# Ordering TensorE together with the other engines, in two lanes, with refitted planner costs

## The chip, the cores and the metric

The kernel runs on one NeuronCore of a Trainium2 chip, with its five engines: TensorE (PE, matrix products), VectorE (DVE), ScalarE (ACT), GpSimd (POOL) and SyncE (SP), which issues most DMAs. The metric is the device time of one execution in microseconds, the median of several runs.

## The reference

What is computed is one layer: a layer norm, attention with 32 heads over a sliding window of 256 positions, and a gated feed-forward network on the same normalised input, whose SiLU scales the attention's output.

```
B, S, D = 1, 2048, 512;  H = 32; Dh = 16; W = 256;  F = 1792
xn = layernorm(x)                                   # no gain, no bias
q, k, v = split(xn @ wqkv)                          # 32 heads of 16
scores = q @ k.T * 16**-0.5
mask = (idx[:, None] - idx[None, :] >= 0) & (idx[:, None] - idx[None, :] < 256)
s = (softmax(where(mask, scores, -1e9)) @ v) @ wo
b = (silu(xn @ w1) * (xn @ w3)) @ w2
out = x + s * silu(b)
```

## The kernel before

**Tiling.** The 2048 tokens are handled in four token tiles (t) of 512, the 32 heads in four head groups (g) of eight, and each pair (t, g) in two passes (p): 32 units of attention. float32 operands are kept as two float16 parts, a rounded one and what the rounding lost, so that a product takes three float16 matmuls (`XH`/`XL` are the parts of the normalised input). Working tiles of 2 KB a partition, for weights, hidden values and residuals alike, are taken from a pool of 46 `slot` buffers.

**Stages.** `prepare` does the layer norm of a tile on DVE: statistics (L422, L423), then a short serial chain on 128x4 numbers, the reciprocal square root by three Newton steps (L427, L430, L431, three times L434 to L436, L437), then the centring of four 128x512 tiles (L440). PE transposes these (L478) and DVE splits them into `XH` and `XL` (L487, L488). `project` (L550) and `value` (L520) make q, k and v; q and k go to DRAM (`dQ`, `dK`, issued at L566, L567, L569, L570) and come back in the layout of the scores (L582). A unit's first pass multiplies queries and keys (PE, L604) for the row maxima, which DVE takes (L616); its second pass makes the scores (PE, L678), DVE adds the mask (L685), ACT takes the exponential into `pt` (L688), and PE multiplies `pt` with the values into the bank `po` (L706). ACT and DVE bring `po` out into `os` (L716, L719), and SP gathers it (L725, L726), fetches the denominators (L739), stores their reciprocals (L743, L744 on DVE, then L746) and spreads them (L750); POOL multiplies (L316), and ACT and POOL split the result (L755, L316).

The feed-forward part runs beside attention. `gate_up` (PE L937) makes gate and up; ACT and DVE finish the hidden value (L948, L952, L957), ACT and POOL split it (L963, L316). `down` (PE L987) sums over pieces of F in a bank and adds it to an accumulator, on ACT for the first piece (L1002) and on DVE for later ones (L1007). From the second token tile on, down goes over `product` (PE L1040, ACT L1050, DVE L1053), which uses operands of half size prepared on POOL. `total` (PE L1118, the last tile by columns at L1153) applies wo, and DVE joins it with x (L1125 to L1127, L1155, L1156). Weights are measured (squares on ACT, L247 and L837), scaled and split (ACT L319, L320; POOL L316) on the way.

**PSUM.** Four kinds of banks stand in the text by tag: `m0` and `m1`, which dense products use in turn (below "dense banks"), `s` with two buffers for scores and small products, and `po` for the values. A matmul that begins a new tile of a bank waits until the tile before it has been read out.

**What sets the order.** `tile_block` emits the program once, in an order written by hand: between two batches of scores it places a share of dense work, and short helpers wait in a list for so many steps (`later`). After that, `arrange` reads the whole program: which instruction must come before which (from the parts of tiles that they touch, `box` and `meets`), how long each takes (`cost`), how long after its end a reader on another engine can start (`extra`), how long a DMA occupies the pipe (`carry`), and by when each must be done so that PE isn't held up (`deadlines`). `listed` then simulates the five engines. PE's instructions stay in the order of the program. Each other engine takes, among those that can begin, the one with the earliest deadline, unless a more urgent one is about to become ready. After three rounds, each of which knows the ready times of the round before, the best order is fixed by dependencies between neighbours on DVE, ACT, POOL and SP; the engines then run their lists strictly in order, waiting on semaphores. So a planner that takes an operation for shorter or longer than it is places it among the wrong neighbours, and everything behind it on that engine waits.

## Time and profile before

| | |
|---|---|
| median of 3 runs | 819.77 us (819.29 to 821.17) |
| profiled execution, its own time | 821.13 us |
| its span, first to last instruction | 819.3 us |
| mean granted TensorE clock | 0.994 |
| first matmul begins / last matmul ends | 1.05 us / 815.6 us |
| PE busy | 797.9 us, 97% |
| DVE busy | 639.2 us, 78% |
| ACT busy | 435.3 us, 53% |
| POOL busy | 358.7 us, 44% |

A row of the timeline gives the start in us, the length in us, the engine, the line of the kernel, the operation, the output, the inputs, the shape and the number of instructions joined in it; in square brackets stands how long the engine had been idle before it, and what ended that. A row of the windows gives for each stretch its length and then, for PE, the weight loads, DVE, ACT and POOL, the busy time and the number of instructions; behind these come the granted TensorE clock (1.00 is full), the share of the DMA engines and the traffic in GB/s. A row of the waits names the engine and the group that waited, what released it, the total in us, how often, and the longest.

### The profile page before, as it was taken

What the parts mean: (1) busy time and instruction counts of PE and PEld (TensorE: products, weight loads), DVE (VectorE), ACT (ScalarE), POOL (GpSimd) and SP (SyncE); (2) the same over time, 40 slices, a digit from 0 to 9 for tenths busy, and PEclk for the clock granted to TensorE, in tenths of its full rate; (3) what the DMA queues carried; (4) which work ended last, traced back from release to release, by engine and by line L of the source; (5) the groups of instructions that cost most, each with busy time, mean ns of one, the idle gap of its engine ahead of it and who ended that gap; (6) DMA issues with size and microseconds to landing.
All of it is one profiled execution on the core that took longest, in us unless ns stands there. A gap on an engine that the chain in (4) does not pass through costs nothing.

```text
span 819.3 us, 23768 instructions
## 1 busy us (share of the span) xinstructions
PE 797.9 (97%) x9088; PEld 415.8 (51%) x9088; DVE 639.2 (78%) x2044; ACT 435.3 (53%) x659; POOL 358.7 (44%) x556
## 2 busy tenths in 40 slices
PE   8999999699999999999999999999999999999998
PEld 4444444344544554454555555545555555545654
DVE  8898889977897777799778866777878787774535
ACT  6898799555636554443443455534443446544421
POOL 2247646672806433523341752514141456435252
PEclk9999999899999999999999999999999999999999
DMA  9996575268665334545364452426375543224521
GB/s 284 284 296 185 164 215 169 75 197 204 176 179 136 117 103 121 152 144 154 106 189 133 125 142 69 140 72 172 112 185 152 159 146 113 56 90 149 172 65 55
DMA packets 112835, 121.99 MB, mean 149 GB/s; under 512 B 18448, under 2 KB 77008, under 8 KB 112720
## 3 DMA queue, kind: packets, MB, share of 16 engines
q1 hardware_dynamic: 112432, 119.94, 51.2%
q8 instruction: 71, 1.16, 0.6%
q10 hardware_dynamic: 288, 0.52, 0.2%
q14 instruction: 44, 0.36, 0.1%
HBM read 83.76 MB, written 32.37 MB: 142 GB/s over the span
## 4 chain that ended last, share of the span: by engine, by line
PE 83%; DVE 12%; issue 2%; DMA 1%; ACT 1%; DVEq 0%; SPq 0%; ACTq 0%
PE m L937 32%; PE m L1040 9%; PE m L550 9%; PE po L706 8%; PE s L678 5%; PE m L1118 5%; PE m L520 5%; PE m L987 4%; DVE junk L616 3%; PE s L604 3%; DVE s L685 2%; PE po L604 2%; DVE st L422 1%; DMA qa<-dQ 1%; DVE slot L957 1%
## 5 line engine op out<-in xcount | busy, mean ns | idle before, releaser
L688 ACT ACTIVATE pt<-s,es 128x1024 f32<-128x1024 f32 x152 | 167.7, 1113 | 198.0 <-DVE s L685 193.3
L937 PE MATMUL m<-XH,slot 128*128 128x512 f16 x896 | 267.4, 380 | 1.0 <-DVE slot L952 0.8
L316 POOL TENSOR_TENSOR slot<-slot,slot 128x256 f16<-128x256 f32 (+1 forms) x222 | 148.6, 696 | 152.4 <-ACT slot L320 66.6
L937 PEld LDWEIGHTS <-slot 128*128 128x128 f16 x1344 | 124.5, 98 | 152.6 <-issue 12.3
L937 PE MATMUL m<-XL,slot 128*128 128x512 f16 x448 | 169.8, 379 | 0.0
L685 DVE TENSOR_TENSOR s<-s,MK 128x256 f32<-128x256 f32 (+2 forms) x280 | 120.7, 437 | 50.4 <-PE s L678 41.9
L616 DVE CUSTOM_DVE_ANT_0 junk<-s,MW 128x320 bf16<-128x320 f32 x276 | 134.5, 487 | 28.0 <-PE s L604 18.6
L906 POOL TENSOR_TENSOR slot<-slot,slot 128x256 f16<-128x256 f32 x133 | 87.9, 685 | 46.4 <-ACT slot L902 46.3
L1040 PE MATMUL m<-slot,slot 128*128 128x256 f16 x798 | 96.4, 276 | 2.0 <-DVE s L685 1.8
L616 DVE CUSTOM_DVE_ANT_0 junk<-po,MW 128x320 bf16<-128x320 f32 x172 | 84.0, 488 | 10.0
L1040 PEld LDWEIGHTS <-slot 128*128 128x128 f16 x798 | 76.9, 99 | 20.4 <-issue 4.5
L706 PE MATMUL po<-pt,V 64*32 64x320 f32 (+4 forms) x2880 | 78.2, 345 | 0.0
L706 PEld LDWEIGHTS po<-pt,V 64*32 64x32 f32 x2880 | 51.9, 106 | 23.8 <-PE s L604 4.0
L910 POOL TENSOR_TENSOR slot<-slot,slot 128x256 f32<-128x256 f32 x19 | 14.2, 747 | 102.8 <-DVE slot L957 96.5
L678 PE MATMUL s<-qa,KA 50*64 50x320 f16 (+3 forms) x1472 | 58.2, 259 | 1.0 <-ACT pt L688 1.0
L987 PE MATMUL m<-slot,slot 128*128 128x512 f16 x216 | 51.6, 386 | 7.0 <-DVE slot L1007 4.7
L952 DVE SCALAR_TENSOR_TENSOR slot<-slot,m 128x512 f32<-128x512 f32 x56 | 38.3, 683 | 24.0 <-ACT slot L948 23.8
L678 PEld LDWEIGHTS <-KA 50*64 50x64 f16 x1472 | 30.2, 105 | 50.9 <-issue 36.3
L716 ACT COPY os<-po 128x512 f32<-128x512 f32 x32 | 18.7, 585 | 70.2 <-PE po L706 70.2
L948 ACT ACTIVATE slot<-m,sgs 128x512 f32<-128x512 f32 x56 | 38.3, 684 | 32.2 <-PE m L937 31.3
L957 DVE SCALAR_TENSOR_TENSOR slot<-m,slot 128x512 f32<-128x512 f32 x56 | 38.5, 687 | 15.9 <-PE m L937 15.5
L604 PE MATMUL s<-KA,qa 48*64 48x320 f16 (+2 forms) x648 | 45.5, 295 | 1.9 <-DVE M L616 0.7
(170 smaller groups left out, 1137.1 us busy)
## 6 DMA issues: line engine op xcount, KB each, us to landing
slot<-dW SPq DMA_DIRECT2D x88, 256.0 KB
slot<-dR SPq DMA_DIRECT2D x56, 256.0 KB
slot<-in_B_w_dram SPq DMA_DIRECT2D x42, 256.0 KB
dW<-slot SPq DMA_DIRECT2D x32, 256.0 KB
slot<-in_A_x_dram SPq DMA_DIRECT2D x30, 256.0 KB
KA<-dK SPq DMA_DIRECT2D x24, 288.0 KB
dR<-slot SPq DMA_DIRECT2D x49, 128.0 KB
qa<-dQ SPq DMA_DIRECT2D x32, 192.0 KB
```

Of the source, the lines that this page charges most:

```text
L316: op(out[:, c], a[:, c], b[:, c])
L550: nc.tensor.matmul(cell["pp"], a[:, k, c, :], b[:, c, :], start=(c, i) == parts[0][0], stop=(c, i) == parts[-1][-1])
L604: nc.tensor.matmul(s[64 * c:64 * c + 64, r, :n], qa[rows, 2 * p + a, ii * P + 64 * c:ii * P + 64 * c + 64], ka[rows, 2 * p + a, e - n:e], ...
L616: nc.vector.tensor_tensor_reduce(out=junk[:, :n], in0=s[:, r, :n], in1=mask, scale=1.0, scalar=NEG, op0=ALU.add, op1=ALU.max, accum_out=M[ ...
L678: nc.tensor.matmul(s[64 * h:64 * h + 64, r, o:o + 64 * n], ka[rows, 2 * p + a, 64 * (m + 4):64 * (m + 5)], qa[rows, 2 * p + a, 64 * (m + k ...
L685: nc.vector.tensor_add(v, v, MK[:, kind, of:of + n, :].unsqueeze(1).to_broadcast([P, 2 * len(which), n, 64]))
L688: nc.scalar.activation(pt, s, AF.Exp, scale=es)
L706: nc.tensor.matmul(cell["po"][32 * i:32 * i + 32, h, 64 * (m + k):64 * (m + k + n)], V[64 * h:64 * h + 64, (4 * t + m // 2) % VB, hd * VW: ...
L906: nc.gpsimd.tensor_sub(made[:, D + c.start:D + c.stop], raw[:, c], made[:, c])
L937: nc.tensor.matmul(cell[k], w[:, (a * NC + c) * P:(a * NC + c + 1) * P], b[:, c, :], start=c == 0 and i == 0, stop=c == NC - 1 and i == 2)
L987: nc.tensor.matmul(ps, hh[:, a * TW + b * P:a * TW + (b + 1) * P], w[:, c * D:(c + 1) * D], start=f == f0 and i == 0, stop=f == f1 - 1 and ...
L1040: nc.tensor.matmul(ps[:, blk, :], l[:, a * D + q:a * D + q + 128], r[:, 256 * c:256 * c + 256], start=f == f0 and x == 0, stop=f == f1 - 2 ...
```

## The change

No instruction is added, taken away or resized. The kernel's text outside the planner is the same; the planner changes in four ways.

1. PE is no longer held to the order of the program. `streams` cuts its instructions into blocks: at most six matmuls of one dense bank, or a run of attention matmuls into one tile. The blocks form two lanes, dense and attention, and each lane keeps its order. `next_block` takes the block that comes first by the order of the round before, unless it isn't ready within 300 ns (`GAIN`), the other lane's next block can begin at least that much earlier, and it stands less than 8 us (`LEADING`) ahead. In the first round the order is the program's. There are four rounds.
2. Durations are refitted: a DMA's issue goes from 420 to 340 ns, ACT from 130 + 0.98n to 30 + 0.9n with additions (n is the elements per partition), DVE gets a floor and forms with two inputs, POOL's simple forms are split from its two-input ones, and a DMA into a few partitions carries more.
3. Delays between engines are refitted (`lag`): by engine instead of one value, 70 ns more for a reader on PE, and a read behind a write on the same engine now counts.
4. `box` computes the part of a tile that an operand touches more tightly; 888 of 11,041 instructions have another set of predecessors through it.

The resulting program has the same 7,456 matmuls. PE's order differs in five places only, where a block has passed others; the other engines' orders differ in many places by a few positions.

**PE, at about 145 us of the profiled execution.** The names `slot21`, `slot2` are parts of w2 as PE's operands for `down`; `m1_2573` and `m0_2679` are its two sums in the dense banks. Before, the 34 attention matmuls of this place (the `x8` rows count each) stand in the second sum, behind its first two blocks of w2 and in front of `slot21`:

```order
L604 LDWEIGHTS qa_1565
L604 MATMUL po_2728<-KA2_142,qa_1565 64x320
L478 MATMUL po_2728<-identf_94,slot10_1530 64x64 x8
L987 LDWEIGHTS slot20_1927
L987 MATMUL m0_2679<-slot21_2366,slot20_1927 128x512
```

Now they stand in the first sum, in front of its last two blocks `slot2` and `slot0` (all buffer numbers are lower by two in the changed program):

```order
L604 LDWEIGHTS qa_1563
L604 MATMUL po_2726<-KA2_140,qa_1563 64x320
L478 MATMUL po_2726<-identf_92,slot10_1528 64x64 x8
L987 LDWEIGHTS slot15_2265
L987 MATMUL m1_2571<-slot2_2457,slot15_2265 128x512
```

So the block with scores `s_2694`, maxima `s_2709` and `po_2728` has moved ahead of twelve L987 matmuls, six of the first sum and six of the second.

**DVE, the same place.** `r0_2849` and `sq_2852` belong to the reciprocal square root of token tile 2, `slot4_1423` is the accumulator that L1007 adds the first sum to. Before, the end of the chain, the centring and L1007 stand like this, with the maxima and masks behind:

```order
L434 TENSOR_TENSOR sq_2852<-r0_2849 128x4
L435 SCALAR_TENSOR_TENSOR sq_2852<-sq_2852,ve_2847 128x4
L436 SCALAR_TENSOR_TENSOR r0_2849<-sq_2852,r0_2849 128x4
L437 TENSOR_SCALAR rs_160<-r0_2849 128x4
L440 TENSOR_SCALAR slot9_2469<-slot9_2469,mv_159,rs_160 128x512
L440 TENSOR_SCALAR slot22_2471<-slot22_2471,mv_159,rs_160 128x512
L1007 SCALAR_TENSOR_TENSOR slot4_1423<-m1_2573,dsc_158,slot4_1423 128x512
L440 TENSOR_SCALAR slot33_2473<-slot33_2473,mv_159,rs_160 128x512
L800 TENSOR_TENSOR p13_157<-pp_2603 128x2
L616 ISA junk_2722,M_2393<-s_2709,MW_111 128x320
```

Now the maxima and the splits of the moved block stand ahead of L1007, and L1007 ahead of the statistics (L422) of tile 2:

```order
L616 ISA junk_2741,M_2391<-po_2726,MW_109 128x320
L616 ISA M_2391 128x1
L487 CAST XH_2299<-po_2726 128x2x128
L487 CAST XH_2299<-s_2707 128x2x128
L1007 SCALAR_TENSOR_TENSOR slot4_1421<-m1_2571,dsc_156,slot4_1421 128x512
L488 TENSOR_TENSOR XL_2300<-po_2726,XH_2299 128x2x128
L488 TENSOR_TENSOR XL_2300<-s_2707,XH_2299 128x2x128
L293 TENSOR_SCALAR pp_2601<-al_2603 128x4
L422 BN_STATS st_2653<-slot9_2467 128x6
```

The chain itself begins some 25 rows later than before and is cut in two by the masks of the next scores `s_2889`; here are the end of its first part and its second part:

```order
L434 TENSOR_TENSOR sq_2850<-r0_2847 128x4
L685 TENSOR_TENSOR s_2889<-s_2889,MK_117 128x4x64
L685 TENSOR_TENSOR s_2889<-s_2889,MK_117 128x2x64
L616 ISA junk_2917,M_2888<-s_2904,M1_104 128x128
L616 ISA M_2888 128x1
L616 ISA junk_2919,M_2888<-s_2904,M1_104 128x128
L616 ISA M_2888 128x1
L487 CAST XH_2299<-s_2904 128x2x128
L1007 SCALAR_TENSOR_TENSOR slot32_1520<-m1_2766,dsc_156,slot32_1520 128x512
L488 TENSOR_TENSOR XL_2300<-s_2904,XH_2299 128x2x128
L435 SCALAR_TENSOR_TENSOR sq_2850<-sq_2850,ve_2845 128x4
L436 SCALAR_TENSOR_TENSOR r0_2847<-sq_2850,r0_2847 128x4
```

L1007 has moved up by 15 rows, the maxima and masks around it by some 30, and the chain L427 to L437 down by 25 to 35.

**SP, at about 570 to 580 us.** `on_9341` is gathered from the two `os` tiles of a unit pair (L725), `dQ1_144` takes projected queries (L566, L567), `dr_9708` fetches the denominators (L739). Before:

```order
L725 DMA on_9341<-os_9338 16x512 x3
L566 DMA dQ1_144<-slot37_9808 128x2x512
L567 DMA dQ1_144<-slot37_9808 128x512
L725 DMA on_9341<-os_9338 16x512
L639 DMA dm_9789<-mt_9787 32x128
L1022 DMA slot44_9920<-dR1_154 128x1024
L1022 DMA slot2_9922<-dR1_154 128x512
L725 DMA on_9341<-os_9700 16x512
L641 DMA qa_8662<-dm_9789 2x1024 x2
L725 DMA on_9341<-os_9700 16x512 x3
L739 DMA dr_9708<-dd_9342 128x32
```

Now the gathers of both `os` tiles and L739 stand ahead of the stores of the queries:

```order
L725 DMA on_9339<-os_9698 16x512 x4
L739 DMA dr_9706<-dd_9340 128x32
L639 DMA dm_9787<-mt_9785 32x128
L566 DMA dQ1_142<-slot37_9806 128x2x512
L567 DMA dQ1_142<-slot37_9806 128x512
L1022 DMA slot44_9918<-dR1_152 128x1024
L641 DMA qa_8660<-dm_9787 2x1024 x2
L1022 DMA slot2_9920<-dR1_152 128x512
L746 DMA de_9837<-dr_9706 128x32
L774 DMA slot34_10091<-dW1_149 128x1024
```

L566 and L567 have moved down by seven places, behind L725 and L739, and L746, which waits for DVE's reciprocals, has come in ahead of two loads.

The diff, cut to its core:

```diff
@@ -1523,40 +1526,50 @@
         if kind == "InstDMACopy":
-            return 420
+            return 340
...
         if i.engine == ENGINE.Activation:
-            return 130 + 0.98 * n + 50 * (len(i.outs) > 1)
+            return 30 + (0 if psum else 30) + 0.9 * n + 95 * scales + 30 * more
         if i.engine == ENGINE.DVE:
-            return 80 + 1.05 * n + (6 * n if kind == "InstReciprocal" else 0) + 45 * (len(i.outs) > 1)
-        return 40 + 2.6 * n
+            return max(160, (185 if inputs > 1 or len(i.outs[0].ap) < 2 or i.outs[0].ap[-1][1] < n else 95) + 0.98 * n + 55 * (scales == 1) + (5 * n if kind == "InstReciprocal" else 0)) - 80
+        return (2.68 * n - 42 if inputs else 0.85 * n) if n > 64 else 100
...
-        return n * size(i.outs[0].dtype) / 300
+        return n * size(i.outs[0].dtype) / (140 if n > 65536 and i.outs[0].ap[0][1] < 64 else 300)
...
-    extra = [1350 + carry(i) if d else 130 if i.engine != ENGINE.PE else 180 for i, d in zip(made, dma)]
+    extra = [1350 + carry(i) if d else {ENGINE.PE: 230, ENGINE.DVE: 140, ENGINE.Activation: 160}.get(i.engine, 100)
+             for i, d in zip(made, dma)]
+
+    def lag(k, a):
+        if made[k].engine == made[a].engine:
+            return extra[k] if (k, a) in reads and made[k].engine != ENGINE.PE else 0
+        return extra[k] + 70 * (made[a].engine == ENGINE.PE)
...
+def streams(made):
+
+    blocks, of = [], {}
+    for k, i in enumerate(made):
+        if i.engine != ENGINE.PE:
+            continue
+        t = i.outs[0].bass_ap.tensor
+        dense = t.tag.startswith("m")
+        b = blocks[-1] if blocks else None
+        if b is None or b[0] != dense or b[1] != t.name or dense and len(b[2]) >= PIECE:
+            blocks.append((dense, t.name, []))
+        blocks[-1][2].append(k)
+        of[k] = len(blocks) - 1
+    return [b[0] for b in blocks], [b[2] for b in blocks], of
...
@@ -1600,23 +1645,42 @@
+        def next_block():
+            able = sorted((lane[h] for lane, h in zip(lanes, heads) if h < len(lane)), key=lambda b: when_of[b])
+            if not able:
+                return None
+            f = free[ENGINE.PE]
+            first = met[able[0]] if not open_[able[0]] else None
+            if len(able) > 1 and (first is None or first > f + GAIN):
+                o = able[1]
+                if not open_[o] and when_of[o] - when_of[able[0]] < LEADING and (
+                        first is None or max(f, met[o]) + GAIN < first):
+                    return max(f, met[o]), o
+            return None if first is None else (max(f, first), able[0])
...
@@ -1645,12 +1709,21 @@
+                if k < 0:
+                    now, at = ~k, 0
+                    taken.append(now)
+                    heads[dense[now]] += 1
+                    k = blocks[now][0]
+                    s = max(s, ready[k])
                 at += 1
-                if SHIFT:
-                    nominal[k] = free[e]
+                if at == len(blocks[now]):
+                    now = None
...
@@ -1659,21 +1732,28 @@
-                when = done + (60 if dma[k] else extra[k] if made[a].engine != e else 0)
+                when = done + (60 + 70 * (made[a].engine == ENGINE.PE) if dma[k] else lag(k, a))
                 margin = AFTER_DMA if dma[k] else AFTER if made[a].engine != e else 0
                 ready[a] = max(ready[a], when, min(when + margin, latest[a] - CLOSE))
+                if a in of:
+                    if of.get(k) != of[a]:
+                        open_[of[a]] -= 1
+                    met[of[a]] = max(met[of[a]], when)
...
-    for e in engines[1:]:
+    for e in engines:
...
-ROUNDS, SHIFT = 3, False
+PIECE, GAIN, LEADING, FOLLOW = 6, 300, 8000, 0.0
+ROUNDS = 4
...
-    with _tile.TileContext(nc) as tc, tc.manual_schedule(engines=ORDERED):
+    with _tile.TileContext(nc) as tc:
```

85 lines of the change are left out of this document (59 added, 26 removed).

## The prediction

> **What bounds the kernel now.** I read the page's busy times and its chain that ended last, then the windows, then the waits, and then the timeline where the windows show a hole.
>
> ```profile
> PE 797.9 (97%) x9088; PEld 415.8 (51%) x9088; DVE 639.2 (78%) x2044; ACT 435.3 (53%) x659; POOL 358.7 (44%) x556
> PE 83%; DVE 12%; issue 2%; DMA 1%; ACT 1%; DVEq 0%; SPq 0%; ACTq 0%
> ```
>
> PE is busy for 797.9 of 819.3 us and carries 83% of the chain. No matmul goes away, so all that a new order can win on PE is 819.3 - 797.9 = 21.4 us of idleness, and whatever a lower clock costs inside the busy time. The windows say where that idleness is.
>
> ```profile
> 0.00:20.00 20.00, 16.57 (x80) 8.09 (x81) 15.92 (x54) 12.92 (x23) 5.51 (x33) 1.00 1.01 284
> 20.00:40.00 20.00, 19.54 (x124) 8.82 (x122) 16.75 (x70) 17.11 (x37) 3.88 (x6) 1.00 0.99 280
> 40.00:60.00 20.00, 20.00 (x138) 8.76 (x137) 18.05 (x73) 19.75 (x46) 9.07 (x14) 1.00 1.01 297
> 60.00:80.00 20.00, 19.20 (x156) 8.69 (x155) 17.93 (x70) 17.46 (x28) 14.85 (x23) 1.00 0.63 181
> 80.00:100.00 20.00, 18.91 (x215) 9.01 (x214) 17.20 (x63) 16.88 (x32) 12.73 (x20) 1.00 0.56 176
> 100.00:120.00 20.00, 19.30 (x201) 8.94 (x202) 16.55 (x61) 17.12 (x33) 8.67 (x15) 1.00 0.73 210
> 120.00:140.00 20.00, 19.71 (x265) 9.95 (x268) 18.22 (x70) 18.38 (x34) 11.63 (x19) 1.00 0.60 184
> 140.00:160.00 20.00, 12.96 (x148) 5.89 (x146) 19.03 (x57) 12.06 (x22) 13.64 (x22) 0.85 0.34 98
> 160.00:180.00 20.00, 19.99 (x226) 9.36 (x212) 15.53 (x53) 11.12 (x19) 18.84 (x29) 0.98 0.49 145
> 400.00:600.00 200.00, 199.64 (x2506) 107.89 (x2505) 157.25 (x487) 92.78 (x124) 74.00 (x109) 1.00 0.44 126
> 600.00:760.00 160.00, 158.06 (x1918) 86.98 (x1916) 118.95 (x357) 75.78 (x102) 73.28 (x109) 0.99 0.46 132
> 760.00:819.30 59.30, 55.59 (x522) 31.27 (x519) 29.48 (x59) 14.47 (x20) 22.96 (x32) 1.00 0.31 93
> ```
>
> The second number of a row is PE's busy time. The stretch 140 to 160 us stands out: 7.04 us idle, a third of all, and the only one whose clock (0.85) is far from full. DVE is busy there for 19.03 of 20 us. From 400 to 600 us only 0.36 us is left; the last 59.3 us lose 3.71, nearly all behind the last matmul.
>
> **The hole at 150 us, the main term.** The timeline:
>
> ```profile
> 138.26 1.46 PE L987 MATMUL m<-slot,slot 128*128 128x512 f16 x6
> 143.83 0.81 PE L987 MATMUL m<-slot,slot 128*128 128x512 f16 x3 [0.65 <-POOL slot L316]
> 147.38 0.38 DVE L427 TENSOR_SCALAR ve<-mv 128x4 f32<-128x4 f32 x1
> 148.43 2.76 PE L987 MATMUL m<-slot,slot 128*128 128x512 f16 x12
> 153.93 0.17 DVE L437 TENSOR_SCALAR rs<-r 128x4 f32<-128x4 f32 x1
> 155.05 0.75 DVE L1007 SCALAR_TENSOR_TENSOR slot<-m,dsc,slot 128x512 f32<-128x512 f32 x1
> 155.85 2.72 PE L987 MATMUL m<-slot,slot 128*128 128x512 f16 x6 [4.66 <-DVE slot L1007]
> 165.48 0.77 DVE L685 TENSOR_TENSOR s<-s,MK 128x256 f32<-128x256 f32 x2 [0.94 <-PE s L678]
> ...
> PE m L987 <- POOL slot L316: 2.0, 5, 0.6
> ```
>
> PE can't begin the next sum of `down` until L1007 has read out the bank. L1007 stands in DVE's list behind the whole reciprocal square root of token tile 2, which runs from 147.38 (L427) to 154.1 us (L437), although the normalised tile isn't wanted yet. PE idles 4.66 us. Then the next six matmuls take 2.72 us, where twelve took 2.76 and six took 1.46 before: half speed. That costs 1.3 us on these six and, by the records up to 160 us, about 0.4 more. Before the hole lie five waits for POOL's splits of w2: 2.0 us of idleness by the list of waits, most of it in the 140 to 147 us that this order spends on one sum. So the stretch loses 7.04 + 1.7 = 8.7 us; that is the upper end of this gain.
>
> The new order does three things here. The 34 attention matmuls now stand between two blocks of the sum that waits for POOL, so they fill those waits. L1007 goes ahead of the statistics and the chain, so the bank is free about when its sum ends. And without a long hole the clock should stay up. What ends last then is DVE: its work of 120 to 180 us hasn't shrunk, and its idle time there is 1.78 + 0.97 + 4.47 = 7.2 us by the rows, of which the part behind 140 us is 5.4. PE can come no earlier at 180 us than DVE serves it, so I take less than 5.4: 4.5 us, since a list in strict order doesn't fill every gap. The lower end is 1 us, two of the five POOL waits filled and nothing else.
>
> The chain doesn't vanish. It goes behind the maxima and in part ahead of the masks (L685) of the next scores. What is it worth there?
>
> ```profile
> L436 DVE SCALAR_TENSOR_TENSOR r<-sq,r 128x4 f32<-128x4 f32 x3 | 1.8, 612 | 0.1
> L435 DVE SCALAR_TENSOR_TENSOR sq<-sq,ve 128x4 f32<-128x4 f32 x3 | 1.8, 588 | 0.1
> L434 DVE TENSOR_TENSOR sq<-r 128x4 f32<-128x4 f32 x3 | 1.4, 469 | 0.1
> 7.91 0.16 DVE L434 TENSOR_TENSOR sq<-r 128x4 f32<-128x4 f32 x1
> ```
>
> The same instruction took 0.16 us at 7.91 us, where POOL was mostly idle (5.51 of 20 us), and 0.47 to 0.61 here. The ten rows of the chain from L427 up to the masks are then worth 10 x 0.16 = 1.6 us beside an idle POOL and 10 x 0.56 = 5.6 beside a busy one. POOL is busy for 18.84 of 20 us from 160 to 180, so I take 5.6 in the place that they move to. That is inside the 4.5, since DVE did the same work at the same price earlier. It is also the seed of the first rival. The Trainium skill, page "GPSIMD Engine Reference", section "1. Specifications", says that POOL shares its SBUF interfaces with VectorE and contends with DVE instructions that have two SBUF inputs or run in a 2-port mode. L434 to L436 have two; the trace agrees, and by that rule the chain is cheap only where POOL rests, which speaks against its new place.
>
> **The smaller terms.**
>
> ```profile
> 9.98 0.19 PE L274 MATMUL s<-sb,onesb 128*128 128x1 bf16 x2 [1.53 <-DVE sb L259]
> 10.03 1.24 PE L1327 MATMUL m<-onesb 128*128 128x512 bf16 x5
> 31.37 0.30 PE L604 MATMUL s<-KA,qa 48*64 48x128 f16 x7 [0.47 <-DMA qa<-dQ]
> ```
>
> At the start the five filler matmuls (L1327, 1.24 us) go into the 1.53 us that PE waits for L259. Behind them PE transposes what DVE has centred, and centring comes slightly later in the new list; between -1.2 and +0.7 I take -0.3. At 31 us six value matmuls go ahead of the scores that wait for `dQ`: -0.4 of the 0.47 idle, and not below. From 60 to 140 us PE loses 0.80 + 1.09 + 0.70 + 0.29 = 2.9 us in eight or so pieces; ACT's fillers stand a few places earlier there and its evacuations later. I take +0.2, between -1 and the second rival's price. The swap at 517 us (six gate matmuls ahead of 52 attention matmuls) has 0.36 us of idleness to work on in 200: nothing, hidden by PE's own queue of ready work; gone, it would cost one DVE mask.
>
> SP at 575 us and at 748 us:
>
> ```profile
> 577.54 1.78 SPq L725 DMA_DIRECT2D on<-os  x3
> ...
> 579.77 1.11 ACT L688 ACTIVATE pt<-s,es 128x1024 f32<-128x1024 f32 x1 [2.64 <-DVE s L685]
> 582.24 1.14 ACT L1092 ACTIVATE slot<-slot 128x512 f32<-128x512 f32 x2
> ...
> 582.77 2.55 PE L706 MATMUL po<-pt,V 64*32 64x256 f32 x96
> 747.69 0.32 SPq L1022 DMA_DIRECT2D slot<-dR  x1
> 750.88 5.33 PE L1040 MATMUL m<-slot,slot 128*128 128x256 f16 x32 [1.79 <-DVE s L685]
> ```
>
> A gather (L725) occupies SP for 1.78 / 3 = 0.59 us, while the planner now takes 0.34. The query stores (L566, L567) go behind up to seven of these and L739, some 4 us later; ACT's L1092 overwrites what they read and now stands ahead of two exponentials (L688) instead of behind them. The first is done at 580.88 and wanted by L706 at 582.77, so 1.9 us are free and 1.14 of them go to L1092 itself. Between 0 and 2 us I take +0.8. At 748 us a load (L1022) that PE's product waits for is issued about 0.5 us later in SP's list: +0.5, between 0 and 1. A dozen moves of L1022 and L1132 by a few places elsewhere: +0.2. At the tail L739 goes behind one more batch of gathers; the last products of the other tile cover it, and without that cover it would be up to +2.
>
> Sum: -0.3 - 0.4 + 0.2 - 4.5 + 0.8 + 0.5 + 0.2 = -3.5 us. Against the profiled execution, 821.13, that gives 817.6. The median of the runs stands 1.36 us lower, at 819.77, and is what I predict from: 816.3.
>
> **The rivals.**
>
> *DVE stays the bound at 150 to 170 us, and the hole moves.* The chain now comes ahead of the masks that PE's next values need (before: 165.48). If PE arrives there 4.5 us earlier, DVE has 5.6 us of chain between maxima and masks, and PE waits for them instead of for L1007. For: DVE was busy 19.03 of 20. Against: the end of the chain is behind the masks, and dense blocks stand between. Only the POOL waits would then be won, about -1: 819.77 - 1 + 1 (the other terms) = 819.8. The Trainium skill, page "TensorE: Matmul & The Clock Gate", section "What's actually happening", says that the clock halves after an idle window of about 3.4 us. The 4.66 us hole and what followed agree. By that rule a moved hole above that length would bring the slow matmuls back, and this rival would hold even with the 1.3 us of clock counted as won.
>
> *ACT falls behind its plan from 40 to 140 us: slower.*
>
> ```profile
> L247 ACT ACTIVATE sqa<-slot x34: 615/629/635, 6.8 to 124.8; 128x512 bf16<-128x512 f32 x34
> L247 ACT ACTIVATION_READ_ACCUMULATOR sqa<-slot x34: 185/187/206, 7.3 to 125.3; 128x1 f32 x34
> 29.51 0.63 ACT L247 ACTIVATE sqa<-slot 128x512 bf16<-128x512 f32 x1
> ...
> 30.27 0.63 ACT L247 ACTIVATE sqa<-slot 128x512 bf16<-128x512 f32 x1
> ```
>
> A square takes 0.63 and up to 0.75 us with the start of its accumulator read (29.51 to 30.27 between two of them); the planner took 0.68 before and takes 0.55 now. With the 14 of L837 that is 48 x 0.14 to 0.20, about 8 us that ACT's plan now lacks, in a stage where ACT is busy 17 to 19.75 of 20 us and PE waits for its evacuations. If all of it reached PE: 819.77 - 3.5 + 8 = 824.3. It decides once more than half of it does (above 821.4). Against: ACT's idle time from 20 to 140 us is 13.3 us, and most evacuations have a second bank.
>
> *The whole hole is won.* POOL waits, L1007 and clock, -8.7, with small terms at +1: 812.
>
> *The change does little.* PE's order differs in five places; if the block at 145 us finds its masks and splits as late as before, 819.8.
>
> **How the numbers follow.** Chances: the forecast 0.46, DVE stays the bound 0.14, ACT behind its plan 0.22, all won 0.12, little 0.06. Within 0.2% (1.64 us, about what can be told from no change) means 818.13 to 821.41. The forecast and all won are faster, 0.58; DVE and little are the same, 0.20; ACT is slower, 0.22. The forecast's own range is 813.5 to 818, from the ends of its terms; the range for 8 in 10 reaches from 811.5, the whole hole won, to 823.5, most of ACT's price.
>
> **What would show it.** Right: the window 140 to 160 us near 18 us of PE, clock 1.00, no wait of PE for L1007 above 1 us, and DVE above 17 us in 160 to 180. Wrong: a PE wait above 2 us for a mask or a split between 150 and 175 us; PE rows of 60 to 140 us below 18.5; a PE wait for `pt` at 582 us or for `dR` at 749 us above 2 us.

## The result, and the profile after: which places gave time and which took it

The new order is slower: 830.45 us in the median (827.80 to 831.66) against 820.38 us (819.29 to 821.17) for the kernel before on the same chip. The ratio is 1.0119, with a 95% interval of 1.0088 to 1.0151. The forecast was 816.3 us, with a range up to 823.5; both the sign and the range were wrong. The profiled execution of after took 831.66 us with a span of 829.9, that of before 821.13 with 819.3.

The page of after begins its list of engines with this row:

```profile
PE 801.1 (97%) x9088; PEld 416.2 (50%) x9088; DVE 638.8 (77%) x2044; ACT 434.0 (52%) x659; POOL 357.1 (43%) x556
```

No work was added on PE, but it is busy 3.2 us longer (801.1 against 797.9), and it idles 28.8 us instead of 21.4. The longer busy time is one of the clock: while PE works, it stands at half for 17.1 us of after's trace and for 10.2 of before's. The windows of after (length, then busy time of PE, PEld, DVE, ACT and POOL, then the granted clock, DMA share and GB/s) say where:

```profile
80.00:100.00 20.00, 15.56 (x177) 7.21 (x176) 15.75 (x55) 15.57 (x28) 15.89 (x25) 0.93 0.60 188
100.00:120.00 20.00, 20.00 (x198) 9.11 (x197) 15.10 (x59) 14.94 (x29) 3.91 (x6) 0.90 0.69 188
140.00:160.00 20.00, 18.41 (x244) 9.47 (x243) 16.92 (x63) 16.89 (x30) 18.64 (x29) 1.00 0.49 142
160.00:180.00 20.00, 14.52 (x117) 6.41 (x115) 19.09 (x54) 8.47 (x14) 16.22 (x25) 0.89 0.43 127
```

The hole at 140 to 160 us is gone: 18.41 us of PE at full clock instead of 12.96 at 0.85. Two holes are new, 80 to 100 us (15.56 instead of 18.91) and 160 to 180 us (14.52 instead of 19.99), and the clock is lowered with each, to 0.93 and 0.90 around the first and 0.89 at the second, which a count of idle time misses.

PE's longest waits in after, by what it waited for (total, times, longest, all in us):

```profile
PE s L678 <- ACT pt L688: 8.2, 4, 2.9
PE m L1118 <- DVE slot L1007: 3.7, 1, 3.7
PE m L1040 <- DMA slot<-dR: 2.2, 1, 2.2
PE m L456 <- DVE slot L440: 2.0, 1, 2.0
PE m L987 <- ACT slot L1002: 1.5, 1, 1.5
```

Both kernels run the same matmuls, so the clearest account is by the start of the same matmul in both traces. The offset is its start in after minus its start in before; the last column is what a stretch added.

| matmul that starts in before at | in after at | offset, us | added in the stretch |
|---|---|---|---|
| 61.66 | 62.93 | +1.27 | +1.3: start of the kernel, and ACT around 55 us |
| 79.76 | 82.28 | +2.52 | +1.25: wait for ACT's L1002 |
| 93.44 | 97.92 | +4.48 | +2.0: statistics chain of one tile ahead of masks |
| 96.76 | 103.78 | +7.02 | **+2.5: the slow matmuls behind that wait** |
| 138.26 | 144.69 | +6.43 | -0.6 |
| 158.94 | 157.16 | -1.78 | **-8.2: the old hole** |
| 167.17 | 164.50 | -2.67 | -0.9 |
| 172.87 | 175.52 | +2.65 | **+5.3: statistics chain of the next tile, and normalising** |
| 176.05 | 181.91 | +5.86 | **+3.2: slow matmuls behind it** |
| 800.07 | 805.05 | +4.98 | -0.9; the median is 6.2 up to 400 us and 6.0 up to 745 |
| 805.03 | 813.85 | +8.81 | **+3.8: the tail's wait** |
| 815.32 | 825.83 | +10.51 | **+1.7: slow matmuls behind it** |

**The old hole.** It was won whole. The timeline of after at that place:

```profile
149.49 0.42 PE L678 MATMUL s<-qa,KA 50*64 50x320 f16 x10 [0.56 <-ACT pt L688]
150.59 6.65 PE L987 MATMUL m<-slot,slot 128*128 128x512 f16 x30
```

Thirty matmuls of `down` run in 6.65 us, 0.22 each, where before they stood in several pieces with 4.66 us of waiting and a stretch at half speed. The eight microseconds are about the prediction's upper bound of 8.7.

**The chain of token tile 2, at 166 us.** The reciprocal square root now stands between scores and their masks (L685), and the next matmuls in PE's list (L678) wait for what follows these masks:

```profile
165.85 1.91 POOL L316 TENSOR_TENSOR slot<-slot,slot 128x256 f16<-128x256 f32 x3
165.94 0.59 DVE L435 SCALAR_TENSOR_TENSOR sq<-sq,ve 128x4 f32<-128x4 f32 x1
168.55 1.11 ACT L688 ACTIVATE pt<-s,es 128x1024 f32<-128x1024 f32 x1 [5.53 <-DVE s L685]
169.72 0.41 PE L678 MATMUL s<-qa,KA 50*64 50x320 f16 x10 [2.68 <-ACT pt L688]
171.81 1.77 DVE L440 TENSOR_SCALAR slot<-slot,mv,rs 128x512 f32<-128x512 f32 x2
174.35 1.11 ACT L688 ACTIVATE pt<-s,es 128x1024 f32<-128x1024 f32 x1 [4.18 <-DVE s L685]
175.52 0.60 PE L678 MATMUL s<-qa,KA 50*64 50x320 f16 x10 [2.06 <-ACT pt L688]
```

PE waits 2.68 us for the chain and 2.06 us for the normalising (L440) that follows it, and from 177 to 182 us matmuls start 0.43 us apart instead of 0.22. The result of this chain isn't read by PE until about 216 us.

**The chain of token tile 1, at 92 us.** The same thing happens in a place that the prediction didn't look at:

```profile
87.74 9.48 POOL L316 TENSOR_TENSOR slot<-slot,slot 128x256 f16<-128x256 f32 x15
94.14 0.59 DVE L435 SCALAR_TENSOR_TENSOR sq<-sq,ve 128x4 f32<-128x4 f32 x1
95.91 0.75 DVE L685 TENSOR_TENSOR s<-s,MK 128x256 f32<-128x256 f32 x2
96.76 1.11 ACT L688 ACTIVATE pt<-s,es 128x1024 f32<-128x1024 f32 x1 [2.85 <-DVE s L685]
97.92 0.64 PE L678 MATMUL s<-qa,KA 50*64 50x320 f16 x10 [2.91 <-ACT pt L688]
98.36 0.14 DVE L435 SCALAR_TENSOR_TENSOR sq<-sq,ve 128x4 f32<-128x4 f32 x1
```

The row of before for an L435 of this chain is:

```profile
89.12 0.16 DVE L435 SCALAR_TENSOR_TENSOR sq<-sq,ve 128x4 f32<-128x4 f32 x1
```

In before the step took 0.16 us, while POOL was idle from 88.5 to 91.2 us. In after it took 0.59 us as long as the fifteen POOL instructions ran, and 0.14 us at 98.36, when they were over. So a chain that was moved by a few microseconds met another engine's burst, and its steps beside that burst became 3.7 times as long. The 2.91 us wait is followed by slow matmuls: the window 98 to 104 us in after has a granted clock of 0.51.

```profile
98.00:104.00 6.00, 6.00 (x30) 2.27 (x30) 5.56 (x23) 3.50 (x7) 0.00 (x0) 0.51 0.73 201
```

**The tail.** In after:

```profile
801.22 3.57 SPq L750 DMA_DIRECT2D rb<-de  x8
807.68 1.41 POOL L316 TENSOR_TENSOR on<-on,rb 128x256 f32<-128x256 f32 x2 [5.11 <-DMA rb<-de]
810.31 0.73 DVE L1093 SCALAR_TENSOR_TENSOR slot<-slot,slot 128x512 f32<-128x512 f32 x1 [4.40 <-ACT slot L1092]
812.92 1.65 DVE L1007 SCALAR_TENSOR_TENSOR slot<-m,dsc,slot 128x256 f32<-128x256 f32 x4
813.85 9.63 PE L1118 MATMUL m<-slot,slot 128*128 128x512 f16 x36 [3.67 <-DVE slot L1007]
```

and in before:

```profile
803.35 0.86 DVE L1007 SCALAR_TENSOR_TENSOR slot<-m,dsc,slot 128x256 f32<-128x256 f32 x2
805.03 7.29 PE L1118 MATMUL m<-slot,slot 128*128 128x512 f16 x33
```

The last product (L1118) needs L1007, whose sums are complete by 810.2 us in after. There it stands in DVE's list behind L1093, which waits for ACT's L1092, behind a POOL product that waits for `rb`, which SP loads late because L739 (`dr<-dd`) was moved behind five gathers (L725). One late DMA holds DVE, and DVE holds PE: 3.67 us of waiting and a slow start of L1118 behind it.

### The profile page after: what moved, and what is told of

Same layout as the page of the kernel before. It is cut to its first block, busy times and chain, and to the rows that moved or that the text cites. A ratio compares the mean times of both kernels' runs of the same rounds, so it can differ in the third digit from the quotient of the medians.

```text
span 829.9 us, 23740 instructions
## 1 busy us (share of the span) xinstructions
PE 801.1 (97%) x9088; PEld 416.2 (50%) x9088; DVE 638.8 (77%) x2044; ACT 434.0 (52%) x659; POOL 357.1 (43%) x556
## 4 chain that ended last, share of the span: by engine, by line
PE 81%; DVE 7%; ACT 3%; POOL 3%; DMA 2%; issue 2%; SPq 1%; DVEq 0%; POOLq 0%; ACTq 0%
PE m L937 32%; PE m L1040 9%; PE m L550 8%; PE po L706 8%; PE s L678 5%; PE m L520 5%; PE m L1118 5%; PE s L604 3%; DVE junk L616 2%; POOL slot L316 2%; PE po L604 1%; PE m L987 1%; DVE s L685 1%; PE m L1327 1%; ACT slot L319 1%
## 5 line engine op out<-in xcount | busy, mean ns | idle before, releaser
L688 ACT ACTIVATE pt<-s,es 128x1024 f32<-128x1024 f32 x152 | 167.8, 1114 | 179.0 <-DVE s L685 174.1
L316 POOL TENSOR_TENSOR slot<-slot,slot 128x256 f16<-128x256 f32 (+1 forms) x222 | 147.5, 697 | 177.1 <-ACT slot L963 41.2
L685 DVE TENSOR_TENSOR s<-s,MK 128x256 f32<-128x256 f32 (+2 forms) x280 | 120.9, 436 | 52.6 <-PE s L678 47.5
L616 DVE CUSTOM_DVE_ANT_0 junk<-s,MW 128x320 bf16<-128x320 f32 x276 | 134.3, 487 | 21.4 <-PE s L604 11.0
L1040 PE MATMUL m<-slot,slot 128*128 128x256 f16 x798 | 94.7, 273 | 2.6 <-DMA slot<-dR 2.2
L678 PE MATMUL s<-qa,KA 50*64 50x320 f16 (+3 forms) x1472 | 58.5, 261 | 8.2 <-ACT pt L688 8.2
L678 PEld LDWEIGHTS <-KA 50*64 50x64 f16 x1472 | 30.6, 106 | 57.9 <-issue 45.8
L987 PE MATMUL m<-slot,slot 128*128 128x512 f16 x216 | 49.5, 379 | 2.6 <-ACT slot L1002 1.5
L902 ACT CAST slot<-slot 128x256 f16<-128x256 f32 (+1 forms) x76 | 40.6, 564 | 18.8 <-DVE slot L957 16.7
L1118 PE MATMUL m<-slot,slot 128*128 128x512 f16 x180 | 43.4, 391 | 3.7 <-DVE slot L1007 3.7
```

The lines of the kernel that those rows point to most:

```text
L316: op(out[:, c], a[:, c], b[:, c])
L616: nc.vector.tensor_tensor_reduce(out=junk[:, :n], in0=s[:, r, :n], in1=mask, scale=1.0, scalar=NEG, op0=ALU.add, op1=ALU.max, accum_out=M[ ...
L678: nc.tensor.matmul(s[64 * h:64 * h + 64, r, o:o + 64 * n], ka[rows, 2 * p + a, 64 * (m + 4):64 * (m + 5)], qa[rows, 2 * p + a, 64 * (m + k ...
L685: nc.vector.tensor_add(v, v, MK[:, kind, of:of + n, :].unsqueeze(1).to_broadcast([P, 2 * len(which), n, 64]))
L688: nc.scalar.activation(pt, s, AF.Exp, scale=es)
L987: nc.tensor.matmul(ps, hh[:, a * TW + b * P:a * TW + (b + 1) * P], w[:, c * D:(c + 1) * D], start=f == f0 and i == 0, stop=f == f1 - 1 and ...
```

## The experiments

All experiments change the planner or the lists that it returns; every kernel computes the whole reference. A ratio is against the kernel before, measured beside it (its median is 819.8 to 820.4 throughout). The kernel after was not run again beside them, so a difference from its 830.45 us is good to some 3 us only. The two traces show the places above. Open was which part of the change makes the list bad, and whether a bad place costs the end of the kernel what it costs locally.

### Lanes or prices: one part of the change at a time

First without the lanes: PE stays in program order, the new prices order the other engines.

```diff
-PIECE, GAIN, LEADING, FOLLOW = 6, 300, 8000, 0.0
+PIECE, GAIN, LEADING, FOLLOW = 6, 300, -1, 0.0
```

> The changed kernel with TensorE's blocks kept in the order of the program (the other lane may never lead), all refitted costs left. Theory A (the refitted costs put DVE's serial chains of 128x4 operations ahead of masks beside a busy POOL, and the tail's multiplications ahead of L1007; the lanes themselves gain at 140 to 160 us): still slower than before, and the gain at 150 us is gone, 826 to 836 us. Rival B (the five passed blocks of TensorE do the harm): back to 818 to 822 us.

Measured: 830.39 us, ratio 1.0109 (1.0088 to 1.0131). That is after's own time without the lanes. PE's longest waits there are of the kind of after's, for an exponential (L688) that comes late:

```profile
PE s L678 <- ACT pt L688: 5.0, 2, 3.6
PE s L604 <- ACT pt L688: 4.6, 3, 3.7
```

So the lanes aren't needed for the loss. The reverse, two lanes with the costs, lags and dependencies of before:

```diff
-            return 340
+            return 420
...
-            return 30 + (0 if psum else 30) + 0.9 * n + 95 * scales + 30 * more
+            return 130 + 0.98 * n + 50 * (len(i.outs) > 1)
...
+    extra = [1350 + carry(i) if d else 130 if i.engine != ENGINE.PE else 180 for i, d in zip(made, dma)]
...
+    def lag(k, a):
+        return extra[k] if made[a].engine != made[k].engine else 0
```

> The two lanes of the changed kernel with the durations, delays and touched parts (cost, extra, carry, box) of the kernel before. Theory A: the chain of token tile 1 stands again where it stood before, so faster than the changed kernel by 5 us or more, 812 to 824 us. Rival B (the lanes do the harm): 827 us or more.

Measured: 831.22 us, ratio 1.0113 (1.0089 to 1.0138). This contradicts the theory that the new prices are what did it: with the old prices and lanes alone the kernel is as slow, at other places, the longest of them this:

```profile
PE s L604 <- DVE NM L621: 4.5, 1, 4.5
```

Either half costs about 10 us alone, and both together cost 10 us. Effects of parts don't add like that. What the two halves have in common is only that they draw a new list.

### Is any new list this bad? One price in the kernel before

To test that, the kernel before, with its one lane and its old prices, was given another price for a DMA issue, which is one number of the planner (420 before, 340 after).

```diff
-            return 420
+            return 400
```

> The kernel before with a single number of its planner changed: a DMA's issue is priced 400 instead of 420 ns. TensorE's order stays as it is; 681 of DVE's 2,044 rows stand elsewhere, most by a few places. Theory E (the list of before is a lucky draw: any new plan, whatever its prices, meets a handful of waits that the planner doesn't see): 824 to 832 us. Theory F (only wrong prices or the lanes do harm): 818 to 822 us, as before.

Measured: 831.45 us, ratio 1.0138 (1.0110 to 1.0166). A price moved by 20 ns shifted 681 of DVE's 2044 rows, and the kernel lost as much as by the whole change. Its longest wait:

```profile
PE m L987 <- DVE slot L1007: 4.0, 1, 4.0
```

The same with 340, the change's own value:

> The kernel before with the one refitted price of a DMA's issue, 340 instead of 420 ns, and nothing else of the change. Theory E (any new plan is worse than the one that was kept): 824 to 832 us. Theory F: 817 to 822 us, since the issues in the trace take 0.3 to 0.6 us and 340 is no worse than 420.

Measured: 836.84 us, ratio 1.0199 (1.0174 to 1.0225), slower even than theory E had it. And with 440:

> The kernel before with a DMA's issue priced 440 instead of 420 ns; this time only 97 of DVE's 2,044 rows, 134 of SP's 899 and none of TensorE's move. Theory E (the kept list is a lucky draw): slower in proportion to what moved, 821 to 828 us. Theory F (a price away from 340 to 420 does no harm by itself): 818 to 821 us.

Measured: 820.52 us, ratio 1.0012 (1.0001 to 1.0023). This list differs from before's in only 97 rows of DVE and 134 of SP, so it is nearly the same list. The time lies in theory F's range and just below theory E's; with so little moved it says little between the two. Last, the kernel after with 360 instead of 340:

> The changed kernel with a DMA's issue priced 360 instead of 340 ns; 585 of DVE's rows and 146 of TensorE's stand elsewhere. Theory E (plans of this planner scatter between 820 and 840 us, whatever the prices): 824 to 838 us. Rival (the changed kernel is a bad draw of a good planner): 812 to 820 us.

Measured: 823.30 us, ratio 1.0041 (1.0026 to 1.0057): 7 us better than after by the same 20 ns. It falls between the two ranges, just below theory E's and above its rival's.

What follows: lists drawn by this planner scatter between 820 and 837 us under edits that say nothing about the machine. Of the lists measured here that came straight from the planner, before's is the fastest, at 819.8 to 820.4, with 820.5 for its near twin; the others took 823.3, 830.4, 830.5, 831.2, 831.5, 833.8 and 836.8. Against such draws a large reordering is likely to be slower, and that can account for the loss without a fault in the lanes or in the new prices. Why before's list is the fastest can't be read from a trace; that it was picked from many by its time would explain it, and wasn't tested.

### A better price for the step that went wrong

The planner of after prices a step of the statistics chain at 109 ns plus 140 ns until the next step may read it, while the trace has 590 where POOL runs. Does the list become good if such a step is priced at 400?

```diff
+        if i.engine == ENGINE.DVE and n <= 32 and kind != "InstISA":
+            return 400
```

> The changed kernel whose planner prices DVE operations of up to 32 elements per partition at 400 ns (with its 140 ns delay 540, about what they take beside a busy POOL) instead of some 80 to 130. Theory A (the underpriced serial chains are the largest part of the loss): the chains stand singly between masks, 816 to 823 us. Theory E: other waits take their place, 824 to 834 us.

Measured: 833.83 us, ratio 1.0160 (1.0126 to 1.0193). No. The waits for `pt` are gone from the top of the list, and others have come, first of all this one:

```profile
PE m L456 <- DVE slot L440: 5.0, 1, 5.0
```

One number can't stand for a step that takes 0.16 us in one place and 0.59 in another. And a new list is a new draw.

### The places of after's list, undone one by one

The following kernels keep after's planner and change its result by hand: a row takes an instruction out of an engine's list and puts it ahead of another one. These are no new draws, so their differences belong to the places that they touch.

```diff
+    for e, k, ahead in MOVES:
+        best_order[e].remove(k)
+        best_order[e].insert(best_order[e].index(ahead), k)
+MOVES = [
+    (ENGINE.DVE, 1394, 1156),
+    (ENGINE.DVE, 1395, 1175),
...
+    (ENGINE.DVE, 1467, 1457),
+]
```

Those seventeen rows take the chain of tile 1 and its normalising apart and spread them, later, over 100 to 121 us, one step between two other instructions. First both chains were spread, the second over 178 to 209 us:

> The changed kernel's lists on all engines, with only the two reciprocal square root chains (token tiles 1 and 2, 17 DVE instructions each) moved later and spread singly between other DVE work, 100 to 121 us and 178 to 209 us of the profiled execution; their readers on TensorE come at 131 and 216 us. Theory A: the waits of TensorE for pt at 98, 170 and 176 us go, with the half clock behind them: 4 + 8 us less, 817 to 820 us. Rival C (DVE is the bound there whatever the order, the hole only moves to the next masks): 826 us or more.

Measured: 825.26 us, ratio 1.0041 (1.0021 to 1.0060). All waits of L678 for `pt` together are now this:

```profile
PE s L678 <- ACT pt L688: 0.9, 2, 0.6
```

The two holes are gone, 7.3 us of idleness, and the kernel is 5.2 us faster than after, about half of what was expected: new small waits came up at 173 to 213 us. Then the chain of tile 1 alone:

> The changed kernel's lists with the chain of token tile 1 alone spread singly over 100 to 121 us. Sum of terms (each place counts by itself): 4.5 us less, 826 us. Theory G (where DVE ends last, TensorE gets back at the next place a part of what it lost at the one before, so the terms don't add): 827 to 829.5 us, and a longer wait for pt at 170 us.

Measured: 824.58 us, ratio 1.0054 (1.0033 to 1.0075), 5.9 us less than after. The hole at 98 us had cost 4.5 by the offsets. So, within the spread of the runs, this cost reaches the end of the kernel undiminished: the surplus that it put on PE isn't refunded later. Then the chain of tile 2 alone, put into gaps in which DVE was idle at 180 to 186 us:

> The changed kernel's lists with the chain of token tile 2 alone in DVE's idle time behind 178 us. Sum of terms: the loss of 8.8 us between 164 and 180 us goes but for a bit, 822 us. Theory G: 824 to 826 us.

Measured: 827.28 us, ratio 1.0094 (1.0065 to 1.0123), 3.2 us less than after where the offsets had 8.5; the interval overlaps after's, so alone this gain isn't secured. The time lies above both forecasts. By the starts of the same matmuls, this trace loses 2.9 us to before between 159 and 218 us, where after's loses 7.9. The trace shows what keeps the 2.9, at a step that had nothing to do with the chain:

```profile
171.41 3.91 DVE L841 CAST sb<-ssq 128x4 bf16<-128x4 f32 x1
```

Sixteen bytes a row, and DVE is held for 3.91 us; PE waits 1.75 and 0.94 us behind it. This comes back below.

The tail, three moves undone (L1007 ahead of L1093 on DVE, a POOL instruction ahead of the products with `rb`, L739 ahead of the gathers on SP):

```diff
+MOVES = [
+    (ENGINE.DVE, 10954, 10941),
+    (ENGINE.Pool, 10901, 10945),
+    (ENGINE.SP, 10793, 10546),
+]
```

> The changed kernel with three moves of the last 30 us taken back: the multiplication L1093 of slot29 behind the two L1007 that it had passed, POOL's split of slot25 ahead of the product with rb, SP's L739 ahead of the gathers. Theory A: TensorE's wait of 3.67 us for L1007 goes, and the half clock behind it: 5 us less, 825 us. Rival D (the tail waits for rb whatever the order): 829 us or more.

Measured: 828.47 us, ratio 1.0089 (1.0059 to 1.0119), 2.0 us less than after. L1118 still waits 2.2 us for L1007, since the DMAs L1101 and L746 had moved on SP too. With these two put back as well:

```diff
 MOVES = [
...
+    (ENGINE.SP, 10972, 10546),
+    (ENGINE.SP, 10886, 10790),
 ]
```

> The changed kernel's lists with the whole tail as it stood before: besides the three moves of the earlier run, SP's L1101 ahead of the gathers and L746 ahead of the last two. Theory A: rb lands 2 us earlier than with the three moves, TensorE's wait for L1007 at the end goes to 0: 824 to 826 us. Rival: the same as with three moves, 828 us.

Measured: 827.15 us, ratio 1.0088 (1.0058 to 1.0117); L1118's wait is gone. The 3.3 us against after are less than the 5.5 of the table, and the intervals overlap. The trace shows why: PE's offset to before stays at 7.9 us from 763 us to the end, so the tail adds nothing, but it enters the tail with 7.9 instead of after's 5.0, since this execution ran at half clock from 759.8 to 763.2 us (after's didn't). That the tail's chain of queues makes the wait is shown; by the medians its size is known only to a few microseconds.

ACT around 55 and 82 us (an evacuation L559 and the scaling L1002 ahead of fillers) and two matmuls at the start ahead of fillers:

```diff
+MOVES = [
+    (ENGINE.PE, 99, 106),
+    (ENGINE.PE, 100, 106),
+    (ENGINE.Activation, 610, 772),
+    (ENGINE.Activation, 962, 940),
+]
```

> The changed kernel's lists with only ACT's L559 at 55 us and L1002 at 82 us ahead of the squares and the exponential, and the two L274 ahead of the five fillers again. Theory A: 1.3 + 1.5 us on ACT's account and about 1 at the start, 826 to 828 us. Theory E in its strong form (the waits move on to the chain at 92 us): 829 us or more.

Measured: 829.72 us, ratio 1.0128 (1.0094 to 1.0163), 0.7 us less than after, which is nothing that can be told. Yet locally it worked: at 80 us the offset to before is 0.35 us instead of 2.5. The next place gave it back:

```profile
98.42 0.64 PE L678 MATMUL s<-qa,KA 50*64 50x320 f16 x10 [5.57 <-ACT pt L688]
```

PE comes 2.2 us earlier to a mask that DVE delivers at the same time, and waits 5.57 us instead of 2.91; by 103 us its offset is 6.6 us, against 7.0 in after. A gain ahead of a place that DVE sets is worth nothing until that place is mended.

### All places mended together

All moves at once (the start, ACT, the chain of tile 1 spread, that of tile 2 into the gaps, the whole tail):

> The changed kernel's lists with a few rows moved by hand: the chain of token tile 1 spread singly over 100 to 121 us, that of token tile 2 into DVE's idle time at 180 to 186 us, two evacuations on ACT (L559 at 55 us, L1002 at 82 us) ahead of the squares and the exponential that they waited behind, two L274 at 9 us ahead of the five fillers again, and the tail's L1093, slot25, L739, L1101 and L746 where they stood before. Theory A (these named places make the whole loss): 829.9 - 8 (chains) - 5 (tail) - 2.5 (ACT) - 1 (start) gives 811 to 817 us, faster than before. Theory E in its strong form (waits only move on): 822 us or more.

Measured: 815.89 us, ratio 0.9944 (0.9926 to 0.9961). That is 14.6 us less than after, and faster than before. The single repairs sum to 5.9 + 3.2 + 3.3 + 0.7 = 13.1 us by the medians, but only to about 9 by the ratios; as each is known to some 3 us, it stays open whether they add up or help each other. One hole is left, at 168 us:

```profile
167.53 4.44 POOL L316 TENSOR_TENSOR slot<-slot,slot 128x256 f16<-128x256 f32 x7
168.09 3.90 DVE L841 CAST sb<-ssq 128x4 bf16<-128x4 f32 x1
172.64 0.59 PE L937 MATMUL m<-XH,slot 128*128 128x512 f16 x2 [1.74 <-DVE slot L563]
```

The small cast begins while seven POOL instructions run back to back and ends with them, at 172.0 us. If POOL holds it, the cast costs nothing in a place where POOL rests. It was moved behind POOL's run, with one more row:

```diff
 MOVES = [
...
+    (ENGINE.DVE, 2559, 2114),
 ]
```

> The version with all hand moves and one more row moved: DVE's cast L841, which took 3.90 us at 168.1 us beside seven POOL splits, goes behind the next masks and maxima, ahead of the chain at 177 us, where POOL rests; its reader on TensorE comes at 191 us. Theory A (POOL's run holds the cast, not the cast's work): the cast takes 0.2 us, TensorE's waits of 1.74 and 0.94 us go: 813 to 814.5 us. Rival (the cast is held by something else): 3.9 us at the new place too, 816 us or more.

Measured: 812.86 us, ratio 0.9912 (0.9887 to 0.9937). This is the fastest version, 7 us ahead of before and 17.6 ahead of after. Its interval overlaps a little with that of the version without the last row, but the traces agree: by 218 us PE is 8.2 us ahead of before, against 5.0 without that row. The same instruction is short now:

```profile
173.88 0.16 DVE L841 CAST sb<-ssq 128x4 bf16<-128x4 f32 x1
```

The two windows that the prediction was about, in this version:

```profile
140.00:160.00 20.00, 19.07 (x274) 10.02 (x267) 17.74 (x62) 15.34 (x26) 19.92 (x32) 1.00 0.35 99
160.00:180.00 20.00, 19.99 (x216) 9.14 (x214) 15.76 (x64) 9.65 (x14) 11.90 (x19) 1.00 0.81 244
```

39.06 us of PE out of 40 at full clock, against 32.95 in before and 32.93 in after. So the old hole can be won without a new one behind it; only the chain has to go where DVE is idle, and the cast to where POOL is.

### The old hole alone, in the kernel before

Last, before's lists with only the move at 150 us: 34 attention matmuls ahead of twelve of `down`, DVE's rows for them and L1007 earlier, the chain of tile 2 in the gap at 180 us.

```diff
+    best_order = {getattr(ENGINE, e): v for e, v in LISTS.items()}
...
+LISTS = {
...
```

> The lists of the kernel before on every engine, with one part of the change alone, set by hand: TensorE's block of 34 attention matmuls at 147 us ahead of the last six L987 of the first sum and six of the second, on DVE the block's masks, maxima and splits and L1007 of slot4 ahead of the weight scales, and the chain of token tile 2 in DVE's idle time at 180 to 186 us. Theory A (the place at 140 to 160 us is a gain of 8 us that the new plan loses elsewhere): 810 to 814 us. Rival (the gain exists only because TensorE ran late there, DVE gives less in the list of before): 816 to 820 us.

Measured: 818.32 us, ratio 0.9968 (0.9956 to 0.9980): faster by 2 us, in the rival's range. At 153 us PE is 7.3 us ahead of before; then 3.1 us are lost at one wait, 1.6 more by 161 us on slow matmuls behind it, and 2.2 between 205 and 242 us. From there to 750 us a lead of only 0.5 us is left in this trace. The other 2.0 us come at 751 to 755 us, where before's execution ran at half clock and this one didn't. The loss at 157 us:

```profile
151.30 1.33 ACT L319 ACTIVATE slot<-slot,pi 128x512 f32<-128x512 f32 x2 [5.32 <-DVE pi L798]
156.99 1.59 PE L706 MATMUL po<-pt,V 64*32 64x320 f32 x28 [2.44 <-ACT pt L688]
```

ACT's list had stayed as it was, so the exponential L688 stood behind L319, which waits for a DVE result of the old order. A block moved on two engines and not on the third kept little of what it won.

## Why the prediction was wrong, step by step

**The hole at 150 us.** The mechanism was right: the block fills the POOL waits, L1007 is early, the clock stays up. Its size was too small, -8.2 against -4.5, close to its bound of 8.7: at this place the rival "the whole hole is won" was right. What the prediction asked to see is there: 18.41 us of PE, clock 1.00, no long wait for L1007.

**"That is inside the 4.5".** This is the step that failed. The chain's new place was priced at 5.6 us and then charged at nothing, because DVE did the same work at the same price before. What counts isn't DVE's total but what stands behind the chain in DVE's list. In before, PE had twelve matmuls of `down` in front of it and lost 4.66 us; in after, the masks of scores stand behind the chain, PE's ready work has been used up by the block that filled the old hole, and the chain, the normalising and the clock cost 8.5. The prediction's own sign of this came: a wait of PE above 2 us for a mask between 150 and 175 us, 2.68 us up to 169.72. The rival "DVE stays the bound, and the hole moves" described this almost exactly, with its sign for: DVE 19.03 of 20. It put the sum at +0, since it won the POOL waits alone, and had 0.14 of the chances. Measured for the two windows together: -8.2 - 0.9 + 8.5 = -0.6.

**60 to 140 us, "+0.2".** This stretch cost about 5.2 us (offset 1.27 at 62 us, 6.43 at 144). Two causes were mixed up in the second rival, which had 8 us of under-priced ACT squares. ACT did fall behind a little, 1.25 us at 82 us and about 0.9 at 56. But the larger part, 4.5, is the other token tile's chain at 92 us, moved beside a POOL burst. The prediction had the prices in hand, 0.16 and 0.56 us a step, and applied them to one of the two chains only. The sign that it named, PE rows below 18.5, came: 15.56. The small term at 31 us came as priced: the offset falls by 0.5 us there, and 0.3 of it are lost again by 38 us.

**The tail, "0, without cover +2".** It cost 5.5 us by the offsets (3.3 by its removal). The cover named, the last products of the other tile, didn't lie between L739 and the end: DVE's L1093 waits for that load's consumers, and it stands ahead of the L1007 that PE needs. The queues were followed to SP and not on through POOL and ACT to DVE.

**The start, "-0.3".** It cost +0.25 by 15 us, and with ACT at 55 us +1.3 by 62 us. The fillers ahead of L274 delayed what DVE needs from it:

```profile
10.12 0.16 DVE L285 TENSOR_SCALAR al<-s 128x1 f32<-128x1 f32 x1 [1.26 <-PE s L274]
12.06 1.08 PE L456 MATMUL m<-identf,slot 128*128 128x128 f32 x8 [2.00 <-DVE slot L440]
```

**SP at 575 and 748 us, "+0.8" and "+0.5"; elsewhere.** At 750.88 us the offset rises by 0.45, the later load, as priced, and the sign named for it came: PE waits 2.24 us for `dR`. Over the next matmuls the offset falls by 1.7, since before ran at half clock from 751.4 to 754.8 us and after didn't, so nothing of it is seen at the end. The stores at 575 us left no step: the median offset is 6.2 us up to 400 us and 6.0 from there to 745.

**The ground of the sum.** It priced five places where PE's order differs and let the rest ride at "elsewhere". The runs show that the rest is the risk: a list for five engines that is drawn anew scatters by 17 us, and before's stood at the fast end. The forecast's 0.46 would have had to be weighed against that, and a trace of one list can't show it. Its range was too narrow even for its own terms: with the second rival left out, their ends add up to -11 and +4.7 us, 808.7 to 824.5, and not to 813.5 to 818.

## What to carry to other kernels

When a planner redraws the lists of several engines, ask of every moved block who stands behind it in each in-order queue, and what it runs beside; one late item costs PE its own wait and, where the clock falls, more through the slow matmuls behind it (1.7 to 3.2 us here). Treat a re-planned order as a new draw, measure several draws before you credit a price or a rule with the difference, and then repair the worst waits by hand: here 44 moved instructions took a list from 830.5 to 812.9 us. Local gains ahead of a place that another engine sets are refunded there, so begin with the places that set the time and mend them together.

## What the runs showed of the hardware

**A running POOL instruction stretches small DVE instructions.** Steps of the chains on 128x4 elements took 0.14 to 0.17 us alone and mostly about 0.59 beside POOL's L316. In after, from 91.9 to 96 us, grouped by shape (busy time, mean ns of one, idle time before):

```profile
L430 DVE TENSOR_SCALAR r<-ve 128x4 int32<-128x4 int32 x1 | 0.6, 594 | 0.0
L436 DVE SCALAR_TENSOR_TENSOR r<-sq,r 128x4 f32<-128x4 f32 x1 | 0.6, 591 | 0.0
```

and from 98 to 104 us, with POOL idle:

```profile
L436 DVE SCALAR_TENSOR_TENSOR r<-sq,r 128x4 f32<-128x4 f32 x2 | 0.3, 160 | 0.0
```

The fifteen POOL instructions at 88 us take 0.63 us each (9.48 / 15), and the steps of the chain beside them begin 0.63 us apart: 92.25, 92.88, 93.52, 94.14, 94.77. Each of them ends within 0.03 us of the end of a POOL instruction, L435 at 94.73 and POOL's at 94.71, so a step here seems to be held until POOL's current instruction is done. One that begins near that end is short: L434 at 163.84 us took 0.18 us beside POOL.

The Trainium skill, page "GPSIMD Engine Reference", section "1. Specifications", names contention with POOL for DVE instructions with two SBUF inputs or in a 2-port mode; the trace agrees for L436, which has two. L430, with one tensor input, took 594 ns in the same stretch; the trace doesn't show in which mode it ran. The 3.9 us of the cast L841 are the strongest case: it waited through seven POOL instructions, and took 0.16 us once moved (the ratio went from 0.9944 to 0.9912 by that one row). Why the cast waited for a whole run of them, and the others didn't, isn't settled.

**What lowered the clock was how little PE did in one stretch of a fixed grid of 3.41 us.** PE waited 2.91 us at 95 to 97.9 us, and the clock of 98 to 104 us was 0.51, some 2.9 us lost on matmuls twice as long. It waited 2.68 us up to 169.72 and the next products were at full speed; then 2.06 us up to 175.52, and matmuls from 177 to 182 us were slow. So the length of a wait alone doesn't decide. The run that moved only the chain of tile 2 keeps the wait at 98 us, and its trace shows it again:

```profile
97.69 0.42 PE L678 MATMUL s<-qa,KA 50*64 50x320 f16 x10 [2.90 <-ACT pt L688]
```

There the clock stayed full. In all 18 traces the clock changes only at the edges of a grid of 3.41 us, full or half, and the windows on that grid tell the two cases apart, after's first and then the two of that trace:

```profile
93.69:97.10 3.41, 1.32 (x7) 0.49 (x5) 3.24 (x9) 0.56 (x2) 3.41 (x6) 1.00 0.78 225
93.21:96.62 3.41, 1.57 (x8) 0.59 (x6) 3.24 (x9) 0.57 (x2) 3.41 (x7) 1.00 0.70 199
96.62:100.03 3.41, 2.20 (x25) 1.09 (x25) 3.09 (x16) 1.59 (x2) 0.36 (x1) 1.00 0.71 217
```

In after 2.1 us of the wait fall into the window that ends at 97.10 us, PE is busy for 1.32 us of it, and the next two windows run at half. In the other trace the edge lies at 96.62 us, so that only 1.8 us of the wait fall into one window, and the clock stays at 1.00. The same holds at 170 us in after: the wait of 2.68 us is split (1.66 and 2.25 us busy), that of 2.06 us is not (1.34). Over all 18 traces, behind the first 5 us, half clock followed 55 windows at full clock, in which PE was busy for 0.00 to 1.62 us. It followed none with more, and six with 1.44 to 1.62 stayed without it. The clock was full again behind a window with 2.88 us or more; up to 2.92 it could stay at half. The grid lies elsewhere in each execution, so a wait near this bound can cost up to 3 us more in one and nothing more in another; how much of the spread between the runs of one kernel comes from that wasn't tested.

The Trainium skill, page "TensorE: Matmul & The Clock Gate", section "What's actually happening", gives an idle window of about 3.4 us. The traces have the same length for the grid, but here a window needn't be idle throughout: up to 1.62 us of work in it didn't keep the clock.
